# A gated mix of two attentions on one core: roundings moved from ScalarE to GpSimd, copies left out, an eleventh query buffer, and single buffers for the output sums

## The chip, the cores and the metric

The kernel runs on one core of a Trainium2 chip. The metric is the device time of one execution, in microseconds (us). Before the change three runs took 1471.78, 1472.81 and 1473.0 us; their median, 1472.81 us, is the time before. The engines are named as the profile names them: PE (TensorE matmul) and PEld (its weight loads), DVE (VectorE), ACT (ScalarE), POOL (GpSimd) and SP (SyncE, which here only issues DMAs). Each engine works through its own instructions in the order in which they were written.

## The reference, cut to what matters

```python
# x: 1 x 2048 x 512, 32 heads of 16
g = sigmoid((x * gate_w).sum(-1, keepdims=True))
# A: each query sees 8 keys: its own position and 2, 4, ... 14 before it
qkv = x @ A_wqkv;  attn = softmax(q . k[idx] / 4, over 8);  a = (attn . v[idx]) @ A_wo
# B: full softmax attention, 32 query heads, one key head and one value head
q = x @ B_wq; k = x @ B_wk; v = x @ B_wv
p = softmax(q @ k.T / 4);  b = (p @ v) @ B_wo
return g * a + (1 - g) * b
```

## The kernel before

Projections run in the matmul's rounded float type (F32R). A factor is split into a high part, which is its rounding, and a low part, which is the rest; three products (high by high, high by low, low by high) stand for the full one. The PE array is used as two halves of 64 rows, and two matmuls, one on each half, run side by side.

**Front** (up to about 278 us). It loads x and the weights, forms the keys `kst`, and then streams 78 projections ("lumps") of 24 half matmuls each: 14 of queries (two more are done ahead), then 64 of branch A, 16 row blocks for each of four column groups `gg`. A query lump ends in `queries_post`: ACT copies the bank to `qraw` (L221, one buffer) and rounds it into `qhi` (L222, three buffers), POOL forms `qlo` (L229, two buffers), and SP stores both parts to the scratch tensor `qd` (L210). `stack` reads them back into one of the query buffers `qst` (ten of them: NB = 9, and `qstx`). A lump of branch A ends in `a_post`: ACT copies the bank into `stage` (L250, two buffers of two lumps), SP stores it to `ad` (L259); in the first group ACT also copies the value columns to `vst` (L252) and the gate's column to `gate` (L253). The weights of the next group are split by `split_wa`: ACT rounds (`wah`, L81), POOL subtracts (`wal`, L82). After the first group `gates` forms the sigmoid, and 16 small ACT copies turn it into `gate_t` (L272).

**Maxima.** Branch B needs the largest score of each query ahead of its exponentials. Its work is cut into 32 units of 4 heads by 512 queries; each needs 64 half matmuls of 512 columns ("fills", 2048 in all). They are put between other matmuls in three forms: a single (L322 into `ps` or `po`, reduced by DVE, L356); a pair (two into `pm`, one reduction, L344); and, in the front and in the output phases, a difference (L393 into `pd`, ACT L405, DVE L417 with a sum into `ps` or `po`), which settles two fills. When a unit's fills are done, `shift_a` to `shift_d` write its maximum into its query buffer: DVE turns it, ACT makes `mh` (L435), POOL `ml` (L442), and eight DMAs carry it (L453), in the front all on SP.

**Blocks** (the following 1167 us). There are 512 steps, 16 key tiles for each of 32 units. A step has two `exp_pair`s (two matmuls into `pe`, L465, and one ACT exponential of 128x1024, L471), four `weighted` matmuls on the step before (L480), one pair of fills, and where `singles` asks for it one single. POOL does branch A's attention beside it from about 145 us on (`a_load` reads `ad` into `aext`, L531).

**Output phases**, after steps 271, 399 and 447: each makes four row blocks of the output. `turn` transposes branch A's rows into a bank, ACT copies it to `raw` (L651) and rounds it (L652), POOL subtracts (L659); `out_store` copies the finished bank to `two` (L678), POOL adds its halves (L681), SP stores (L682). Four row blocks are left for the end, where ACT and DVE copy the last one half each (L1318, L1319).

**The planner.** The order of all engines is fixed when the program is built. `clk` holds a planned time for PE, ACT and DVE and `pool` one for POOL; each written instruction moves them on by a constant, and `pick`, `side_fill` and `singles` take a fill where the planned clocks allow it. A change of a planned cost so moves fills.

## Time and profile before

| | |
|---|---|
| median of three runs | 1472.81 us |
| the profiled execution | 1471.12 us, span 1469.1 us, TensorE clock 1.000 |
| busy: PE, DVE, ACT, POOL | 99%, 78%, 89%, 65% of the span |
| first exponential of the blocks, end of the last | 278.6 us, 1445.3 us |
| 1024 exponentials of 128x1024 (L471) | 987.8 us in all |

A row of a view of groups reads: line, engine, operation, what is written and read, count, then busy time in us, mean ns of one, idle time of that engine just ahead of them and what ended it. A row of the timeline reads: start in us, length in us, engine, line, operation, written and read, count, and in brackets the idle time ahead of it and its releaser. A row of the waits reads: who waited for whom, us in all, times, longest. PE's ends are modelled, so PE's busy share alone does not say that it was full.

### The profile page before, as it was taken

The numbers are of one execution on the slowest core, as the hardware profiler recorded it, in microseconds if no ns is written. First come the engines' busy times: TensorE is split into PE (matmuls) and PEld (weight loads), VectorE is DVE, ScalarE is ACT, GpSimd is POOL, SyncE is SP. The second block draws the span as 40 slices with busy tenths as digits, with TensorE's granted clock in tenths as the row PEclk, the third lists the DMA queues.
The fourth block names the chain that finished last, engine by engine and source line by source line (L and its number), as shares of the span: only waits on it lengthen the run. The fifth ranks groups of instructions, "written<-read, shape, count | busy, mean of one in ns | idle before, by whom it ended". The sixth has DMA issues, their size and how long they took to land.

```text
span 1469.1 us, 29512 instructions
## 1 busy us (share of the span) xinstructions
PE 1454.6 (99%) x10965; PEld 739.7 (50%) x10965; DVE 1141.9 (78%) x1837; ACT 1303.6 (89%) x1706; POOL 951.1 (65%) x1693
## 2 busy tenths in 40 slices
PE   9999999999999999999999999999999999999998
PEld 6899999733333333333333373333333743383334
DVE  6778888788888888788888877888888778778821
ACT  5888988799999999999999989999999889889994
POOL 5731898888988988889888898898851311150000
PEclk9999999999999999999999999999999999999999
DMA  6653342320211210102202111121100000000000
GB/s 225 170 169 113 101 149 68 117 73 25 71 41 49 78 49 31 68 22 69 78 12 71 42 63 46 45 71 41 42 12 12 27 16 2 1 31 1 1 2 29
DMA packets 43912, 85.67 MB, mean 58 GB/s; under 512 B 9520, under 2 KB 25960, under 8 KB 39672
## 3 DMA queue, kind: packets, MB, share of 16 engines
q1 hardware_dynamic: 36632, 44.79, 9.9%
q0 software_dynamic: 6560, 37.95, 7.7%
q8 instruction: 86, 1.41, 0.4%
q10 hardware_dynamic: 576, 1.05, 0.2%
q14 instruction: 58, 0.48, 0.1%
HBM read 57.97 MB, written 25.25 MB: 57 GB/s over the span
## 4 chain that ended last, share of the span: by engine, by line
PE 94%; ACT 2%; POOL 1%; DVE 1%; DMA 1%; issue 1%; SPq 0%; POOLq 0%; ACTq 0%
PE po L480 34%; PE pe L465 25%; PE pf L1082 10%; PE pm L322 8%; PE ps L322 5%; PE pe L780 5%; PE pd L393 3%; PE po L322 1%; ACT pexp L471 1%; PE pf L193 1%; PE pe L1283 1%; DMA ad<-stage 0%; DVE mx L344 0%; DMA xraw<-xt 0%; PE pm L836 0%
## 5 line engine op out<-in xcount | busy, mean ns | idle before, releaser
L471 ACT ACTIVATE pexp<-pe 128x1024 f32<-128x1024 f32 x1024 | 987.8, 1023 | 67.6 <-PE pe L465 63.3
L344 DVE TENSOR_REDUCE mx<-pm 128x2 f32<-128x1024 f32 x475 | 580.1, 1221 | 174.6 <-PE pm L322 172.3
L480 PE MATMUL po<-pexp,vst 128*32 128x512 f32 x4096 | 545.5, 605 | 0.1
L465 PE MATMUL pe<-qst,kst 64*128 64x512 f32 x1984 | 523.3, 459 | 4.6 <-ACT pexp L471 2.5
L465 PEld LDWEIGHTS pe<-qst,kst 64*128 64x128 f32 x1984 | 208.8, 183 | 451.6 <-ACT pexp L471 427.2
L405 ACT ACTIVATE dd<-pd 128x512 f32<-128x512 f32 x367 | 209.0, 604 | 44.7 <-PE pd L393 30.9
L356 DVE TENSOR_REDUCE mx<-ps 128x1 f32<-128x512 f32 x333 | 226.5, 680 | 4.5 <-PE ps L322 1.8
L322 PE MATMUL ps<-kst,qst 62*128 62x512 f32 x503 | 206.5, 410 | 0.1
L322 PE MATMUL pm<-kst,qst 62*128 62x512 f32 x916 | 185.9, 397 | 0.4
L542 POOL TENSOR_TENSOR pr<-aext 128x256 f32<-128x256 f32 x256 | 182.0, 737 | 4.9 <-DMA aext<-ad 4.6
L602 POOL TENSOR_TENSOR oa<-oa,av 128x256 f32<-128x256 f32 x224 | 164.1, 732 | 15.8
L480 PEld LDWEIGHTS po<-pexp,vst 128*32 128x32 f32 x4096 | 80.6, 108 | 170.3 <-issue 161.8
L417 DVE CUSTOM_DVE_ANT_0 dd<-ps,dd 128x512 f32<-128x512 f32 x185 | 127.7, 690 | 34.2 <-PE ps L322 14.2
L417 DVE CUSTOM_DVE_ANT_0 dd<-po,dd 128x512 f32<-128x512 f32 x182 | 125.6, 690 | 29.8 <-PE po L322 12.9
L599 POOL TENSOR_TENSOR av<-aext,lg 128x256 f32<-128x256 f32 x224 | 139.3, 622 | 12.8
L393 PE MATMUL pd<-kd,qst 62*128 62x512 f32 x367 | 143.5, 401 | 2.5 <-ACT dd L405 2.5
L1082 PE MATMUL pf<-wal,xh 64*128 64x384 f32 (+1 forms) x496 | 127.9, 338 | 0.0
L1082 PE MATMUL pf<-wah,xh 64*128 64x384 f32 (+1 forms) x496 | 124.0, 337 | 0.0
L1082 PE MATMUL pf<-wah,xl 64*128 64x384 f32 (+1 forms) x496 | 122.7, 338 | 0.0
L322 PEld LDWEIGHTS ps<-kst,qst 62*128 62x128 f32 x503 | 92.9, 185 | 43.5 <-DVE mx L356 38.6
L506 POOL TENSOR_TENSOR rl<-rl,gate_t 128x16 f32<-128x16 f32 x31 | 6.9, 222 | 157.9 <-DVE rl L500 157.9
L322 PEld LDWEIGHTS pm<-kst,qst 62*128 62x128 f32 x916 | 88.3, 186 | 3.5 <-DVE mx L344 3.0
(199 smaller groups left out, 1725.4 us busy)
## 6 DMA issues: line engine op xcount, KB each, us to landing
aext<-ad POOLq DMA_DIRECT2D x32, 1056.0 KB, 5.4
ad<-stage SPq DMA_DIRECT2D x32, 384.0 KB
qst<-qd SPq DMA_DIRECT2D x62, 128.0 KB
xraw<-xt SPq DMA_DIRECT2D x16, 256.0 KB
qd<-qhi SPq DMA_DIRECT2D x16, 256.0 KB
qd<-qlo SPq DMA_DIRECT2D x16, 256.0 KB
qst<-qd SPq DMA_DIRECT2D x62, 64.0 KB
qst<-ml SPq DMA_DIRECT2D x220, 2.0 KB
```

The source lines that it names most:

```text
L322: nc.tensor.matmul(dst, qst[place(v)][b:b + 62, pr, t * P:(t + 1) * P], kst[b:b + 62, kc * 512:(kc + 1) * 512], start=True, stop=True)
L344: got = nc.vector.tensor_reduce(m[:, :, pr, t, kc], dst, AX.X, ALU.max)
L356: got = nc.vector.tensor_reduce(m[:, odd, pr, t, kc:kc + 1], dst, AX.X, ALU.max)
L393: nc.tensor.matmul(dst, qst[place(v)][b:b + 62, pr, t * P:(t + 1) * P], kd[0][b:b + 62, kc // 2, :], start=True, stop=True)
L405: got = nc.scalar.activation(held[b][k], dst, AF.Relu)
L417: got = nc.vector.tensor_tensor_reduce(held[b][k], dst, held[b][k], 1.0, -FMAX, ALU.add, ALU.max, m[:, b, pr, t, kc:kc + 1])
L465: nc.tensor.matmul(bank[:, odd, :], kst[b:b + 64, kt * P:(kt + 1) * P], qst[place(u)][b:b + 64, pr, :], start=True, stop=True)
L471: got = nc.scalar.activation(e, bank, AF.Exp, scale=SCALE)
L480: nc.tensor.matmul(po[32 * i:32 * i + 32, :], vst[:, kt, :], pexp[s, i // 2][:, i % 2, :], start=(kt == 0), stop=(kt == NJ - 1))
L542: nc.gpsimd.tensor_mul(pr[:, k], q, e[:, o:o + NH, AC:2 * AC])
L602: nc.gpsimd.tensor_add(ao, ao, av)
L1082: inst = nc.tensor.matmul(home(x)[0][:, :n], l[h], r[h], start=(i == 0 and b == 0), stop=(i == 3 * C - 1 and b == 1))
```

## The change

- `split_wa`: the rounding of the 16 weight pieces moves from ACT to POOL, ahead of POOL's subtraction; the planned cost is 1800 ns, not 1100.
- `queries_post`: ACT only copies the bank to `qraw`; POOL rounds it into `qhi` and then subtracts. The planned cost is 0.62 us on ACT, not 1.1, and 2300 ns on POOL, not 1400.
- `a_post` and `gates`: value and gate columns are copied together into `vst`, the sigmoid reads its column from there, and POOL sets that column back to ones. The 16 copies to `gate_t` become 16 DMAs on SP, and `gate_t` has another layout, which its three readers follow.
- A query buffer `qsty` is allocated at the start of the blocks; `place` and `gone` count with eleven, and the stack of unit 10 moves to step 2.
- `turn`: no copy to `raw`; DVE subtracts, straight out of the bank in PSUM.
- `two` and `os` have one buffer in place of two; the splits of the output weights are written ahead of the next load.
- LEAD is 1.75 for 1.5; the last row block is copied by ACT alone.

```diff
-        split(wah[gg][:, c, :n], wal[gg][:, c, :n], waraw.pop((gg, c))[:, :n], nc.gpsimd)
-        pool = max(pool, clk["pe"] * 1e3) + 1100
+        hi, lo, src = wah[gg][:, c, :n], wal[gg][:, c, :n], waraw.pop((gg, c))[:, :n]
+        nc.gpsimd.tensor_copy(hi, src)
+        nc.gpsimd.tensor_sub(lo, src, hi.bitcast(F32))
+        pool = max(pool, clk["pe"] * 1e3) + 1800
...
-        nc.scalar.activation(hi, bank, AF.Copy)
-        at = after("act", clk["pe"] + T_LAT, 1.1)
-        mark(got, at - 0.45, ups_at)
+        at = after("act", clk["pe"] + T_LAT, 0.62)
+        mark(got, at, ups_at)
...
+            nc.gpsimd.tensor_copy(hi, own)
             nc.gpsimd.tensor_sub(lo, own, hi.bitcast(F32))
-            pool = max(pool, 1e3 * at) + 1400
+            pool = max(pool, 1e3 * at) + 2300
...
-            nc.scalar.activation(vst[:, j, 0:DH], bank[:, GN:GN + DH], AF.Copy)
-            nc.scalar.activation(gate[:, 1, j:j + 1], bank[:, GN + DH:GN + DH + 1], AF.Copy)
-        at = after("act", clk["pe"] + T_LAT, 0.5 if gg else 0.9)
+            nc.scalar.activation(vst[:, j, 0:DH + 1], bank[:, GN:GN + DH + 1], AF.Copy)
+        at = after("act", clk["pe"] + T_LAT, 0.5 if gg else 0.7)
...
-        nc.scalar.activation(gate[:, 0, :], gate[:, 1, :], AF.Exp, scale=-1.0)
+        nc.scalar.activation(gate[:, 0, :], vst[:, :, DH], AF.Exp, scale=-1.0)
+        nc.gpsimd.memset(vst[:, :, DH:DH + 1], 1.0)
...
-        nc.scalar.activation(gate_t[i:i + 32, :, :, b], gate[32 * b:32 * b + 32, 1, :].rearrange("p (q j) -> p q j", j=4), AF.Copy)
-        after("act", 0, 0.24)
+        nc.sync.dma_start(gate_t[i:i + 32, b], gate[32 * b:32 * b + 32, 1, :])
...
-        return v if v <= NB else (v - NB - 1) % (NB - 2)
+        return v if v <= NB + 1 else (v - NB - 2) % (NB - 2)
...
-        return v - NB - 1 if v < 2 * NB - 1 else v - NB + 2
+        return v - NB - 2 if v < 2 * NB else v - NB + 2
...
-        own = pe[0].tile([P, 2, C, 64], F32, name="raw", bufs=1)
-        nc.scalar.activation(own, src, AF.Copy)
         nc.scalar.activation(hv, src, AF.Copy)
-        free[f"e{k}"] = after("act", at, 1.3)
+        ready = after("act", at, 0.65)
...
-            nc.gpsimd.tensor_sub(lv, own, hv.bitcast(F32))
-            pool = max(pool, 1e3 * clk["act"]) + 1300
+            nc.vector.tensor_sub(lv, src, hv.bitcast(F32))
+            free[f"e{k}"] = after("dve", ready + 0.1, 0.74) + 0.1
...
-        two = p2b[0].tile([P, 2, D], F32, name="two", bufs=2)
+        two = p2b[0].tile([P, 2, D], F32, name="two", bufs=1)
...
+    qst.append(pe[0].tile([P, 2, 512], F32R, name="qsty"))
+    clear(NB + 1, nc.gpsimd)
...
-        elif k < 3:
+        else:
             nc.scalar.activation(os, banks[k], AF.Copy)
-        else:
-            nc.scalar.activation(os[:, 0:256], banks[k][:, 0:256], AF.Copy)
-            nc.vector.tensor_copy(os[:, 256:512], banks[k][:, 256:512])
```

The lower planned cost on ACT moves fills. Counted in the order of the PE queue, 576 of the 2048 fills stand ahead of the first exponential before and 606 after; the steps hold 323 singles before and 291 after; the three output phases hold 185 fills before and 184 after, and the rest are pairs. The phases stay at steps 271, 399 and 447. The number of matmuls is the same.

The first place is PE in step 137, the tenth of unit 8. Before (`pe` are the banks of the exponentials, `pm` takes a pair and `ps` a single, `po` sums the weighted values of the step ahead):

```order
L480 MATMUL po_88<-pexp_4273,vst_72 32x512 x2
L480 MATMUL po_88<-pexp_4300,vst_72 32x512 x2
L465 MATMUL pe0_4182<-qst8_84,kst_71 128x512 x2
L322 MATMUL pm_4178<-kst_71,qst4_80 128x512 x2
L322 MATMUL ps_87<-kst_71,qst4_80 128x512
L465 MATMUL pe1_4183<-qst8_84,kst_71 128x512 x2
```

The step holds a pair and a single. After, the same step on PE:

```order
L481 MATMUL po_88<-pexp_4311,vst_72 32x512 x2
L481 MATMUL po_88<-pexp_4351,vst_72 32x512 x2
L466 MATMUL pe0_4228<-qst8_84,kst_71 128x512 x2
L323 MATMUL pm_4224<-kst_71,qst4_80 128x512 x2
L466 MATMUL pe1_4229<-qst8_84,kst_71 128x512 x2
```

The step has lost its single; over all steps 32 singles fewer are left.

The second place is POOL in the front, from the first streamed query lump on. Before (`qst` rows are the clearing of query buffers, `waraw` the load of a weight piece):

```order
L229 TENSOR_TENSOR qlo_375<-qraw_373,qhi_374 128x512
L163 MEMSET qst4_80 32x1024 x2
L229 TENSOR_TENSOR qlo_429<-qraw_427,qhi_428 128x512
L163 MEMSET qst5_81 32x1024 x2
L131 DMA waraw_492<-wa 128x402
L229 TENSOR_TENSOR qlo_489<-qraw_487,qhi_488 128x512
```

After, on the same queue:

```order
L230 CAST qhi_374<-qraw_373 128x512
L231 TENSOR_TENSOR qlo_375<-qraw_373,qhi_374 128x512
L165 MEMSET qst4_80 32x1024 x2
L230 CAST qhi_427<-qraw_426 128x512
L231 TENSOR_TENSOR qlo_428<-qraw_426,qhi_427 128x512
L165 MEMSET qst5_81 32x1024 x2
L131 DMA waraw_486<-wa 128x402
L230 CAST qhi_483<-qraw_482 128x512
L231 TENSOR_TENSOR qlo_484<-qraw_482,qhi_483 128x512
```

A CAST stands ahead of each subtraction; the clearings stay where they were.

The third place is SP at the shift of unit 5, in branch A's third column group. Before (`ml` rows carry a unit's maximum, `stage` rows store projections):

```order
L259 DMA ad_69<-stage_2833 128x4x192
L453 DMA qst5_81<-ml_2934 2x8x32 x4
L259 DMA ad_69<-stage_2935 128x4x192
L453 DMA qst5_81<-ml_2934 2x8x32 x4
L259 DMA ad_69<-stage_3045 128x4x192
```

After, where POOL issues the next `aext` load directly behind its `ml`:

```order
L260 DMA ad_69<-stage_2772 128x4x192
L454 DMA qst5_81<-ml_2799 2x8x32 x8
L260 DMA ad_69<-stage_2878 128x4x192
L260 DMA ad_69<-stage_2984 128x4x192
L260 DMA ad_69<-stage_3081 128x4x192
```

All eight DMAs of the shift now stand ahead of the next store. The 16 DMAs to `gate_t` stand on SP among the shifts of units 3 and 4 and the stores around them.

More of the change, by code (lines that the diff above doesn't have):

```diff
@@ L41 @@
 NH = NJ // 2
-LEAD, M2S, M1S, MARGIN = 1.5, 0.5, 0.3, 0.12
+LEAD, M2S, M1S, MARGIN = 1.75, 0.5, 0.3, 0.12
 T_R, T_LAT, T_EXP, T_RED2, T_RED1, T_W, T_TTR = 0.235, 0.20, 0.92, 1.14, 0.61, 1.21, 0.74
@@ L63, in gated_mix_kernel @@
     gate = cp.tile([P, 2, NJ], F32, name="gate")
-    gate_t = cp.tile([P, NQB, 4, 4], F32, name="gate_t")
+    gate_t = cp.tile([P, 4, NJ], F32, name="gate_t")
     mk = cp.tile([P, 8], F32, name="mk")
@@ L505, in finish_b @@
             charge(950)
-        eng.tensor_mul(rl, rl, gate_t[:, qb].rearrange("p j b -> p (j b)"))
+        rv = rl.rearrange("p (j b) -> p j b", b=4)
+        eng.tensor_mul(rv, rv, gate_t[:, :, 4 * qb:4 * qb + 4].rearrange("p b j -> p j b"))
         eng.tensor_mul(obp["t"][:, :, hg % 2, :], tt[:, :, 0:DH], rl.unsqueeze(2).to_broadcast([P, 4 * 4, DH]))
@@ L622, in wo_load @@
     def wo_load(k, c):
-        wot[k, c] = p2b[0].tile([P, 512], F32, name="os", tag="two", bufs=2)
+        wot[k, c] = p2b[0].tile([P, 512], F32, name="os", tag="two", bufs=1)
         nc.sync.dma_start(wot[k, c], (wo_a, wo_b)[k][c * P:(c + 1) * P, :])
@@ L947, in gated_mix_kernel @@
     for i in range(2 * C + 1):
[L948 to L949 removed]
+        wos.append([(wo_split, kcs[i - 1])] if i else [])
+        wos[-1] += [(wo_load, kcs[i])] if i < 2 * C else []
     def work():
@@ L1229, in gated_mix_kernel @@
         u, kt = divmod(s, NJ)
-        if len(stacked) < NU and s >= 16 * (gone(len(stacked)) + 1):
+        if len(stacked) < NU and s >= max(2, 16 * (gone(len(stacked)) + 1)):
             stack(len(stacked))
```

11 lines of the change are left out of this document (5 added, 6 removed).

## The prediction, made before the changed kernel was run

> **What bounds the kernel now.** I read the page first.
>
> ```profile
> PE 1454.6 (99%) x10965; PEld 739.7 (50%) x10965; DVE 1141.9 (78%) x1837; ACT 1303.6 (89%) x1706; POOL 951.1 (65%) x1693
> ...
> PE 94%; ACT 2%; POOL 1%; DVE 1%; DMA 1%; issue 1%; SPq 0%; POOLq 0%; ACTq 0%
> ```
>
> PE is busy throughout and holds 94% of the chain. But its ends are modelled, so the next view is the busy time by stage: a stretch with POOL's early work, one of branch A's projections, and one of the blocks.
>
> ```profile
> 24.00:60.00 36.00, 35.74 (x267) 30.36 (x267) 28.81 (x69) 27.64 (x53) 32.19 (x30) 1.00 0.55 154
> ...
> 100.00:146.00 46.00, 46.00 (x477) 45.76 (x476) 37.56 (x114) 38.55 (x102) 7.33 (x13) 1.00 0.34 106
> 500.00:600.00 100.00, 100.00 (x705) 35.91 (x708) 81.90 (x100) 94.37 (x104) 87.80 (x174) 1.00 0.13 43
> ```
>
> In the front (second row) weights load for 45.76 of 46 us while ACT and DVE have idle time: PE is the limit. In the blocks PE and ACT (94.37) are both near full, so I look at single steps there. These rows are the starts of five steps on PE, and the waits name what ACT lacks:
>
> ```profile
> 501.02 0.50 PE L465 MATMUL pe<-qst,kst 64*128 64x512 f32 x2
> ...
> 503.20 0.50 PE L465 MATMUL pe<-qst,kst 64*128 64x512 f32 x2
> ...
> 505.35 0.50 PE L465 MATMUL pe<-qst,kst 64*128 64x512 f32 x2
> ...
> 507.24 0.50 PE L465 MATMUL pe<-qst,kst 64*128 64x512 f32 x2
> ...
> 509.37 0.50 PE L465 MATMUL pe<-qst,kst 64*128 64x512 f32 x2
> ```
>
> ```profile
> ACT pexp L471 <- PE pe L465: 63.3, 279, 1.7
> ```
>
> The steps take 2.18, 2.15, 1.89 and 2.13 us. The third alone holds no single fill; there ACT runs its two exponentials without a gap. A single makes the step wait for PE. So fills cost differently by place, and the change moves them.
>
> **The change, part by part.**
>
> *Singles out of the blocks.* 323 become 291, 32 fewer. The waits price one: 63.3/279 = 0.227 us of idle ACT. 32 x 0.227 = 7.3 us less. The four steps give 2.153 - 1.89 = 0.26, or 8.3, as the far end. The near end comes from ACT's small work, which the idle time in steps with a single can hide:
>
> ```profile
> L435 ACT ACTIVATE mh<-mt,mk 128x32 fp32r<-128x32 f32 x32 | 10.4, 325 | 0.1
> ...
> L572 ACT ACTIVATE lg<-lg 128x128 f32<-128x128 f32 x32 | 10.0, 311 | 0.0
> ```
>
> If 32 of 512 steps no longer hide it, 20.4 x 32/512 = 1.3 us show, so 6.0. I take 7.3, the price over 279 cases.
>
> *More fills in the front.* 576 become 606, 30 more, between matmuls that already fill PE. The groups of 100 to 146 us:
>
> ```profile
> L1082 PE MATMUL pf<-wah,xl 64*128 64x402 f32 x86 | 22.8, 342 | 0.0
> ...
> L393 PE MATMUL pd<-kd,qst 62*128 62x512 f32 x54 | 21.3, 394 | 0.0
> L1082 PE MATMUL pf<-wah,xh 64*128 64x384 f32 x38 | 10.9, 335 | 0.0
> ...
> L322 PE MATMUL po<-kst,qst 62*128 62x512 f32 x27 | 10.7, 396 | 0.0
> ...
> L1082 PE MATMUL pf<-wah,xl 64*128 64x384 f32 x36 | 9.5, 335 | 0.0
> ```
>
> There are three groups of 86 with 402 columns, 54 + 27 + 27 fills with 512 (the two 27 read alike), and 111 matmuls with 384 (groups of 38, 37 and 36), 201,636 columns in 46 us. A fill takes 512/201,636 of that, 0.117 us, as two halves run at once. 30 x 0.117 = +3.5 us. The ends are +2 (some fall into gaps) and +7 (each keeps the other half idle).
>
> *ACT relieved in the front.* The groups that go or shrink:
>
> ```profile
> L222 ACT ACTIVATE qhi<-pf 128x512 fp32r<-128x512 f32 x14 | 8.4, 598 | 0.0
> ...
> L81 ACT ACTIVATE wah<-waraw 128x384 fp32r<-128x384 f32 (+1 forms) x16 | 8.6, 537 | 0.1
> ...
> L272 ACT ACTIVATE gate_t<-gate 32x16 f32<-32x16 f32 x16 | 3.6, 228 | 0.4
> ```
>
> That is 20.6 us off an engine that is not the limit: worth nothing beyond the fills it lets in, priced above.
>
> *Rounding on POOL.* 14 query roundings and 16 weight roundings are added to a queue that was busy for 32.19 of 36 us between 24 and 60 us. ACT may write `qraw` again only when POOL has subtracted, so POOL's pace now counts. Its rows, with the cast's duration from the end of the kernel, a weight subtraction, and two ACT copies:
>
> ```profile
> 37.71 1.29 POOL L229 TENSOR_TENSOR qlo<-qraw,qhi 128x512 fp32r<-128x512 f32 x1
> 39.05 1.93 POOL L163 MEMSET qst<- 32x1024 f32 x2
> ...
> 44.30 0.62 POOL L131 DMA_DIRECT2D waraw<-wa  x1
> ```
>
> ```profile
> L803 POOL CAST qst<-ob x3: 609/611/613, 1222.0 to 1387.9; 128x512 fp32r<-128x512 f32 x3
> ```
>
> ```profile
> L82 POOL TENSOR_TENSOR wal<-waraw,wah 128x384 fp32r<-128x384 f32 (+1 forms) x16 | 15.2, 949 | 34.6 <-ACT wah L81 34.6
> ```
>
> ```profile
> 39.03 0.60 ACT L221 ACTIVATE qraw<-pf 128x512 f32<-128x512 f32 x1
> ...
> 59.59 0.59 ACT L221 ACTIVATE qraw<-pf 128x512 f32<-128x512 f32 x1
> ```
>
> POOL's first pair now ends at 37.7 + 0.61 + 1.29 = 39.6, so the second copy, due at 39.03, waits 0.6. Up to the sixth pair POOL has six pairs (11.4), five clearings (9.7), two loads (1.2) and one weight pair (0.95 and 402/512 of a cast, 1.4): it ends at 61.4, where the seventh copy was due at 59.59. Later the clearings are over and POOL catches up. I take +1.5 us, between 0 (PE has four banks to run ahead in) and +2.2. The second group's weight roundings have room (POOL was busy for 7.33 of 46 us); the later ones, with a planned cost above their own, defer branch A's work instead of being late.
>
> The Trainium skill (SBUF — State Buffer, on the port that VectorE and GpSimd share) says that a VectorE instruction in a two-port mode, or with two SBUF inputs, shuts a GpSimd instruction out until it ends. By that a cast could take longer than 0.61; the three casts here, within 4 ns of each other in a stretch where DVE is busy, don't show it.
>
> *The stores behind the shifts.* The front's one long stall:
>
> ```profile
> 205.34 0.25 POOL L442 TENSOR_TENSOR ml<-mt,mh 128x32 fp32r<-128x32 f32 x1
> ...
> 207.92 0.57 POOL L531 DMA_DIRECT2D aext<-ad  x1
> ```
>
> ```profile
> 205.62 2.61 SPq L453 DMA_DIRECT2D qst<-ml  x4
> 208.34 0.36 SPq L259 DMA_DIRECT2D ad<-stage  x1
> ```
>
> ```profile
> 215.56 0.49 ACT L250 ACTIVATE stage<-pf 128x384 f32<-128x384 f32 x1 [2.94 <-DMA ad<-stage]
> ```
>
> SP's four DMAs waited for a late `ml`; the store behind them was issued 0.4 us after a load into `aext` and landed 7.2 us later, and ACT stood for 2.94 us. In the new order the store stands behind eight DMAs, planned later in the row pair, and POOL's branch A work is deferred, so `ml` should be less late. I take the stall as gone, less 0.6 for the gate DMAs on SP (one such ahead of a store, 2.61/4): -2.3, with ends -2.9 and +2.9 (one more of its kind).
>
> *Phases and end.* `two` has one buffer:
>
> ```profile
> 859.67 1.03 ACT L678 ACTIVATE two<-pe 128x1024 f32<-128x1024 f32 x1 [0.19 <-PE pd L393]
> ...
> 867.85 1.03 ACT L678 ACTIVATE two<-pe 128x1024 f32<-128x1024 f32 x1
> ```
>
> ```profile
> 862.93 0.37 SPq L682 DMA_DIRECT2D out<-two  x1
> ```
>
> The store has 4.9 us to land before the next copy. I count nothing; if it took the 7.2 us seen above, the copy would be 2.3 us late. The Trainium skill (Trainium Kernel Development and Optimization, Best Practices) asks for double buffers to overlap DMA with compute and so speaks against this part. In `turn` ACT and POOL lose an instruction each and DVE gets four subtractions a phase:
>
> ```profile
> L818 DVE TENSOR_TENSOR qst<-pm,qst x4: 691/692/693, 1400.7 to 1406.7; 128x512 fp32r<-128x512 f32 x4
> ...
> 1464.70 0.38 ACT L1318 ACTIVATE osl<-ps 128x256 f32<-128x256 f32 x1 [4.60 <-PE ps L1310]
> ...
> 1465.12 0.42 DVE L1319 COPY osl<-ps 128x256 f32<-128x256 f32 x1 [6.27 <-ACT osl L1318]
> ```
>
> 4 x 0.69 = 2.8 us a phase lie beside PE's work, with fills as many as before (185, now 184): 0, ends -1 and +2.8. The two halves of the last copy ran one behind the other, 0.84 us; one copy of 512 columns takes 0.60 (L221 above): -0.2. The eleventh buffer, the order of the weight splits and LEAD move no phase: 0.
>
> *Sum*: -7.3 + 3.5 + 1.5 - 2.3 - 0.2 = -4.8. The profiled execution took 1471.12, below all three timed runs, so 1466.3 in its terms; on their median of 1472.81 it is **1468.0 us**. I call 0.2%, 2.9 us, the least that a measurement tells from no change; faster then means under 1469.9, slower over 1475.7.
>
> **The rivals.**
>
> *The gain is eaten.* The stage stall recurs once (no -2.3) and POOL's queue costs its upper end: -7.3 + 3.5 + 2.2 - 0.2 = -1.8, 1471.0. For it: the pattern of late `ml`, SP, and store is all still there. Against: POOL's deferred work.
>
> *Slower by stores behind shifts.* If late shifts and gate DMAs push the store in front of the second, third and fourth group into `aext` loads, each costs 2.94. Without the -2.3 the sum is -2.5 with one such stall, as before; two make +0.4, three +3.4, which is 1476.2. It decides from three on. For it: six shifts fall into this stretch. Against: the trace has one.
>
> *Casts held up.* If each cast waits for one DVE instruction of 0.69, the seventh copy is 6 x 0.69 = 4.1 us later: -4.8 + 4.1 = -0.7, 1472.1. The Trainium skill's page SBUF — State Buffer would make this case.
>
> *One sum buffer waits.* If every store lands only after 7.2 us, the three copies of each phase that have a predecessor wait 2.3 us: 9 x 2.3 = 20.7, 1488.7. Such a landing was seen only beside a large load, and two of the phases come after those. The Trainium skill's Best Practices (Trainium Kernel Development and Optimization) would make this case.
>
> **How the numbers follow.** Forecast 0.60; gain eaten 0.24; casts held up 0.05; three stalls 0.08; sum buffer 0.03. Faster is the forecast, 0.60; same is the two middle ones, 0.29; slower 0.11. The range for 8 in 10 leaves out the last two and a little below: its upper end, 1473.5, holds the eaten gain and the held casts with some spread; its lower end, 1463.5, is the forecast with singles at 8.3, the front's fills at +2, and the queue at 0 (4 us less) and a little spread.
>
> **What would show it.** Exponentials should start about 3 us later or less than before; ACT's wait for PE ahead of exponentials should have some 250 cases, not 279; the query copies should wait for `qlo`, below 2 us each; the wait for the stage store should be gone; the copies into `two` should wait for no DMA. I am wrong if the first exponential comes more than 6 us later, if the steps without a single take longer than 1.9 us, or if the copy into `two` waits for a DMA.

## The result, and the profile after

The changed kernel took 1466.63 us (median of six runs, 1465.39 to 1469.46) beside 1472.89 us before (six runs, 1470.65 to 1473.33): a ratio of 0.9962, with a 95% interval of 0.9952 to 0.9972. A second set of five runs gave 1467.31 us and 0.9968 (0.9955 to 0.9980). So it is faster by 0.3 to 0.4% (0.2 to 0.5% by the intervals); 1468.0 us was forecast. Two executions, one of experiment 9 (1553.73 us at a clock of 0.85) and one of the kernel before (2234.95 us at 0.56), were slow and are left out of every ratio.

The first profiled run took 1469.46 us, the longest of its six, with a granted clock of 0.997. The second took 1466.83 us at 0.999, and it is the one read here unless said otherwise. Its page:

```profile
PE 1452.1 (99%) x10965; PEld 741.2 (51%) x10965; DVE 1140.7 (78%) x1844; ACT 1294.1 (88%) x1647; POOL 956.5 (65%) x1714
...
PE 92%; POOL 2%; ACT 1%; issue 1%; DVE 1%; DMA 1%; SPq 0%; POOLq 0%; ACTq 0%
```

ACT's busy time fell by 9.5 us, POOL's rose by 5.4, and PE holds 92% of the chain, where it held 94%. Three spans add up to the difference of the two profiled executions, 4.1 us. The first exponential starts here, before the change and then after it:

```profile
278.56 1.03 ACT L471 ACTIVATE pexp<-pe 128x1024 f32<-128x1024 f32 x1 [0.72 <-PE pe L465]
```

```profile
280.88 1.03 ACT L472 ACTIVATE pexp<-pe 128x1024 f32<-128x1024 f32 x1 [1.06 <-PE pe L466]
```

| us | before | after | difference |
|---|---|---|---|
| start to first exponential | 278.6 | 280.9 | +2.3 |
| first exponential to the end of the last | 1166.7 | 1160.75 | -6.0 |
| end of the last exponential to the end | 23.8 | 23.4 | -0.4 |

(The first profile had +2.6, -3.7 and -0.4.) The front became longer, and the blocks won more. What ACT waits for, in a view of the waits after:

```profile
ACT pexp L472 <- PE pe L466: 55.5, 248, 1.4
...
ACT qraw L223 <- POOL qlo L231: 4.4, 4, 2.5
...
ACT stage L252 <- DMA ad<-stage: 4.2, 4, 2.1
```

In the first row, 279 cases and 63.3 us have become 248 and 55.5: 31 fewer, at 0.224 us each. The second row is POOL's queue, which hardly held ACT before (0.4 us, once). The third is the stall that the prediction had as gone: there are four of them now (one, of 1.5 us, in the first profile).

**A ledger of the front.** The prediction had a pace for PE there, 46 us for 201,636 columns. What a stretch takes beyond its columns at that pace is its shortfall. All 78 lumps are the same in every kernel; only the fills differ. The stretches run from the first query copy to the first stage copy (query lumps), from there to the 17th stage copy (first group), and to the 57th (later groups). Each cell has fills / length / shortfall, worked out from the records of PE and ACT in one trace of each kernel.

| | query lumps | first group | later groups | shortfall |
|---|---|---|---|---|
| before | 125 / 55.9 / 1.9 | 111 / 48.2 / 0.2 | 304 / 125.3 / 5.5 | 7.6 |
| changed | 140 / 58.3 / 2.6 | 124 / 51.1 / 1.6 | 306 / 122.1 / 2.2 | 6.4 |
| old planned costs | 125 / 58.5 / 4.5 | 111 / 48.2 / 0.2 | 304 / 124.6 / 4.9 | 9.6 |
| queries rounded on ACT | 125 / 54.9 / 1.1 | 126 / 50.3 / 0.2 | 305 / 121.1 / 1.4 | 2.7 |
| the same, order of the changed | 140 / 59.4 / 3.8 | 124 / 51.5 / 1.9 | 306 / 122.1 / 2.2 | 7.9 |
| before, queries rounded on POOL | 140 / 59.3 / 3.7 | 111 / 49.8 / 1.7 | 305 / 123.6 / 3.9 | 9.3 |
| weights rounded on ACT | 140 / 59.3 / 3.7 | 124 / 51.3 / 1.8 | 306 / 123.2 / 3.1 | 8.6 |

Busy time by stretch shows the same. Before the change, 34 to 74, 74 to 145 and 145 to 245 us (columns: PE, PEld, DVE, ACT, POOL, clock, DMA share, GB/s):

```profile
34.00:74.00 40.00, 39.77 (x332) 35.56 (x331) 30.95 (x88) 34.48 (x68) 30.21 (x33) 1.00 0.58 160
74.00:145.00 71.00, 71.00 (x714) 69.47 (x714) 57.29 (x174) 60.43 (x151) 17.24 (x24) 1.00 0.45 138
145.00:245.00 100.00, 97.70 (x1006) 94.88 (x1004) 84.63 (x254) 87.83 (x184) 87.10 (x173) 1.00 0.37 114
```

After it:

```profile
34.00:74.00 40.00, 38.95 (x323) 32.61 (x322) 32.91 (x94) 31.47 (x59) 36.58 (x44) 1.00 0.57 157
74.00:145.00 71.00, 69.90 (x690) 67.79 (x688) 61.01 (x182) 58.69 (x129) 22.18 (x34) 1.00 0.41 119
145.00:245.00 100.00, 100.00 (x1041) 98.19 (x1043) 87.88 (x264) 86.03 (x165) 88.22 (x166) 1.00 0.40 125
```

PE lost 0.8 us in the first stretch and 1.1 in the second, and won 2.3 in the third; the weight loads (PEld) went from 94.88 to 98.19 of 100 us there.

### The profile page after: what moved, and what is told of

Read it like the earlier page. It is cut to its first block, busy times and chain, and to the rows that moved or that the text cites. A ratio compares the mean times of both kernels' runs of the same rounds, so it can differ in the third digit from the quotient of the medians.

```text
span 1467.7 us, 29483 instructions
## 1 busy us (share of the span) xinstructions
PE 1453.2 (99%) x10965; PEld 741.7 (51%) x10965; DVE 1140.8 (78%) x1844; ACT 1293.9 (88%) x1647; POOL 954.3 (65%) x1714
## 4 chain that ended last, share of the span: by engine, by line
PE 92%; POOL 3%; issue 2%; ACT 1%; DVE 1%; DMA 1%; SPq 0%; POOLq 0%; ACTq 0%
PE po L481 33%; PE pe L466 24%; PE pf L1083 10%; PE pm L323 8%; PE ps L323 5%; PE pe L781 4%; PE pd L394 3%; PE po L323 2%; ACT pexp L472 1%; POOL xl L82 1%; PE pe L1286 1%; DVE mx L345 0%; DMA xraw<-xt 0%; POOL tr L550 0%; DMA ad<-stage 0%
## 5 line engine op out<-in xcount | busy, mean ns | idle before, releaser
L466 PE MATMUL pe<-qst,kst 64*128 64x512 f32 x1920 | 497.5, 461 | 5.3 <-ACT pexp L472 3.1
L466 PEld LDWEIGHTS pe<-qst,kst 64*128 64x128 f32 x1920 | 197.4, 184 | 446.6 <-ACT pexp L472 415.3
L406 ACT ACTIVATE dd<-pd 128x512 f32<-128x512 f32 x382 | 222.5, 601 | 52.9 <-PE pd L394 27.8
L357 DVE TENSOR_REDUCE mx<-ps 128x1 f32<-128x512 f32 x302 | 205.5, 680 | 3.6 <-PE ps L323 3.1
L323 PE MATMUL ps<-kst,qst 62*128 62x512 f32 x467 | 191.0, 409 | 0.3 <-DVE mx L418 0.2
L418 DVE CUSTOM_DVE_ANT_0 dd<-ps,dd 128x512 f32<-128x512 f32 x193 | 133.1, 690 | 28.3 <-ACT dd L406 7.8
L1083 PE MATMUL pf<-wal,xh 64*128 64x384 f32 (+1 forms) x496 | 148.0, 338 | 0.0
L418 DVE CUSTOM_DVE_ANT_0 dd<-po,dd 128x512 f32<-128x512 f32 x189 | 130.4, 690 | 19.7 <-PE po L323 9.4
L1083 PE MATMUL pf<-wah,xh 64*128 64x384 f32 (+1 forms) x496 | 145.5, 338 | 0.0
L1083 PE MATMUL pf<-wah,xl 64*128 64x384 f32 (+1 forms) x496 | 141.8, 337 | 0.0
L323 PEld LDWEIGHTS ps<-kst,qst 62*128 62x128 f32 x467 | 86.7, 186 | 32.0 <-DVE mx L357 26.1
L1083 PEld LDWEIGHTS pf<-wal,xh 64*128 64x128 f32 x496 | 90.8, 186 | 0.2
```

The source lines that it names most:

```text
L323: nc.tensor.matmul(dst, qst[place(v)][b:b + 62, pr, t * P:(t + 1) * P], kst[b:b + 62, kc * 512:(kc + 1) * 512], start=True, stop=True)
L357: got = nc.vector.tensor_reduce(m[:, odd, pr, t, kc:kc + 1], dst, AX.X, ALU.max)
L406: got = nc.scalar.activation(held[b][k], dst, AF.Relu)
L418: got = nc.vector.tensor_tensor_reduce(held[b][k], dst, held[b][k], 1.0, -FMAX, ALU.add, ALU.max, m[:, b, pr, t, kc:kc + 1])
L466: nc.tensor.matmul(bank[:, odd, :], kst[b:b + 64, kt * P:(kt + 1) * P], qst[place(u)][b:b + 64, pr, :], start=True, stop=True)
L1083: inst = nc.tensor.matmul(home(x)[0][:, :n], l[h], r[h], start=(i == 0 and b == 0), stop=(i == 3 * C - 1 and b == 1))
```

## The experiments

Edits are against the changed kernel unless said otherwise. (The expectations count 190 fills in the output phases of the changed kernel, where the count above has 184: they take in one pair beside each phase.)

**1. The changed kernel once more.** 

> The changed kernel itself, profiled once more. The first profile of it had a TensorE clock of 0.997 and was the longest of its runs (1469.46 us against a median of 1466.63); in it the stretch from the first to the last exponential was only 3.7 us shorter than before (1163.0 against 1166.7), where the prediction had 7.3 for the singles taken out. Theory 1 (each single taken out of the blocks is worth 0.227 us of ACT waiting for PE): at a clock of 1.000 that stretch is 7 us shorter than before, 1159.5, and the first exponential stays at 281.2. Rival (ACT's small work eats half of it): the stretch stays at 1162 to 1163 and the missing 3 us come from the front, whose first exponential is then at 278 to 279.

Measured: 1467.31 us, the blocks 1160.75, the first exponential at 280.88. That is Theory 1's front, and blocks between the two, nearer to Theory 1. Five other kernels with 291 singles bound it: their blocks took 1159.4, 1159.8, 1160.2, 1160.6 and 1161.8 us (experiments 6, 7, 12, 9 and 8, the last with a clock of 0.997), 4.9 to 7.4 less than before.

**2. Old planned costs, new operations.**

```diff
-        at = after("act", clk["pe"] + T_LAT, 0.62)
-        mark(got, at, ups_at)
+        at = after("act", clk["pe"] + T_LAT, 1.1)
+        mark(got, at - 0.45, ups_at)
...
-            pool = max(pool, 1e3 * at) + 2300
+            pool = max(pool, 1e3 * at) + 1400
```

(1800 and 0.7 in `split_wa` and `a_post` went back to 1100 and 0.9 as well.) 

> The changed kernel with the planner's old costs (1.1 us on ACT and 1400 ns on POOL for a query lump, 0.9 us for a lump of the first branch A group, 1100 ns for a weight piece). All operations stay those of the changed kernel, so ACT, POOL and the stores are relieved or loaded as in it; only fills move: 578 in the front for 606, 307 singles in the blocks for 291, 964 fills in pairs for 961, 199 in the output phases for 190. Theory 1 (fills moved): -28 x 0.117 = -3.3 us in the front, +16 x 0.227 = +3.6 in the blocks, +9 x 0.117 = +1.1 in the phases, so +1.4 us, 1468.0; the first exponential is 3.3 us earlier than in the changed kernel, at 278. ACT's waits for PE ahead of exponentials have some 268 cases, not 254. Rival (the relief of ACT itself is worth something and the front's fills are free): the front stays as long as in the changed kernel, 281, and the time is 1466.6 + 3.6 + 1.1 = 1471.3.

Measured: 1472.02 us, ratio 1.0001 (0.9992 to 1.0010): the whole gain is gone although every operation is the changed one. The first exponential is at 281.69, where Theory 1 had 278. The time is the rival's, but not its reason: the ledger shows 30 fills fewer, worth 3.5 us, and 3.2 us more shortfall (9.6 for 6.4), so the front gains nothing, and the blocks take 1165.1 us, 4.4 more. In the query lumps POOL rounds, and a plan that takes it for faster than it is runs into it: a query copy waits 2.90 us for POOL, up to 58.43 us, and PE pauses for 2.0 us of the 10 between 50 and 60. What holds PE back in the later groups (4.9 short for 2.2) was not followed. The stretches:

```profile
34.00:74.00 40.00, 38.00 (x306) 34.20 (x304) 28.75 (x82) 27.28 (x51) 36.05 (x44) 0.96 0.58 156
74.00:145.00 71.00, 71.00 (x710) 70.22 (x709) 57.40 (x172) 56.00 (x126) 23.96 (x36) 1.00 0.44 125
145.00:245.00 100.00, 97.50 (x1014) 95.08 (x1012) 85.38 (x257) 82.58 (x161) 89.58 (x178) 1.00 0.39 121
```

The first row has a clock of 0.96; it was 0.83 between 60 and 70 us, which may account for up to 0.17 x 10 = 1.7 us of that stretch's shortfall.

**3. Without the eleventh buffer.**

```diff
-        return v if v <= NB + 1 else (v - NB - 2) % (NB - 2)
+        return v if v <= NB else (v - NB - 1) % (NB - 2)
...
-        return v - NB - 2 if v < 2 * NB else v - NB + 2
+        return v - NB - 1 if v < 2 * NB - 1 else v - NB + 2
...
-    qst.append(pe[0].tile([P, 2, 512], F32R, name="qsty"))
-    clear(NB + 1, nc.gpsimd)
...
-        if len(stacked) < NU and s >= max(2, 16 * (gone(len(stacked)) + 1)):
+        if len(stacked) < NU and s >= 16 * (gone(len(stacked)) + 1):
```

> The changed kernel without the eleventh query buffer (placement and stacking times as before the change). The front keeps its 606 fills; the blocks have 301 singles for 291, 944 fills in pairs for 961, 197 in the phases for 190. The prediction counted the buffer as nothing by itself. Theory 1 (fills moved): +10 x 0.227 + 7 x 0.117 = +3.1 us, 1469.7, with the first exponential at the same time and some 263 waits of ACT for PE. Rival (only the front's fills matter): no change, 1466.6.

Measured: 1471.40 us, 0.9992 (0.9983 to 1.0001). The front is the same (281.07; shortfall 6.4), the blocks take 1165.15. So 10 singles more and 17 fills fewer in pairs go with 4.1 us, more than the 3.1 forecast, and without this buffer next to nothing of the gain remains.

**4. LEAD at 1.5.**

```diff
-LEAD, M2S, M1S, MARGIN = 1.75, 0.5, 0.3, 0.12
+LEAD, M2S, M1S, MARGIN = 1.5, 0.5, 0.3, 0.12
```

> The changed kernel with LEAD at 1.5 as before the change. The prediction said that LEAD moves no phase; in fact with 606 fills in the front the third output phase then comes after step 463 and not 447, and the blocks have 277 singles for 291, 963 fills in pairs for 961, 197 in the phases for 190. Theory 1 (fills moved): -14 x 0.227 + 7 x 0.117 = -2.4 us, 1464.2, unless the later phase comes too late for the end. Rival (a phase 16 steps later hands its wait to the end or loses its fills): 1467 to 1470.

Measured: 1471.67 us, 1.0000 (0.9991 to 1.0008). Theory 1 missed by 7.5 us. From the first exponential up to the end of the second phase the two traces agree within 0.3 us; then the third phase comes 16 steps later, and the fills that it would have taken are due before it:

```profile
1301.41 1.22 PE L466 MATMUL pe<-qst,kst 64*128 64x512 f32 x4 [1.77 <-DVE mx L345]
1302.25 1.94 ACT L472 ACTIVATE pexp<-pe 128x1024 f32<-128x1024 f32 x2 [5.17 <-PE pe L466]
```

Ahead of this step, 456, the planner's `pause` writes fills into the exponentials' own banks; the step takes 7.11 us, and ACT waits 5.17. So the kernel before has its third phase at step 447 with a LEAD of 1.5, but with the new fills it takes 1.75 to keep it there, and that is worth some 4 us.

**5. Query roundings back on ACT.**

```diff
-        at = after("act", clk["pe"] + T_LAT, 0.62)
-        mark(got, at, ups_at)
+        nc.scalar.activation(hi, bank, AF.Copy)
+        at = after("act", clk["pe"] + T_LAT, 1.1)
+        mark(got, at - 0.45, ups_at)
...
-            nc.gpsimd.tensor_copy(hi, own)
             nc.gpsimd.tensor_sub(lo, own, hi.bitcast(F32))
-            pool = max(pool, 1e3 * at) + 2300
+            pool = max(pool, 1e3 * at) + 1400
```

> The changed kernel with the query roundings back on ACT, at their old planned costs (1.1 us on ACT, 1400 ns on POOL); everything else stays. The order then has 592 fills in the front for 606, 301 singles in the blocks for 291, 964 fills in pairs for 961. The changed kernel took 1466.6 and 1467.3 us. Theory 1 (fills moved, and PE held up by POOL in the query lumps): -14 x 0.117 = -1.6 in the front, -1.1 for PE time that the longer POOL queue cost between 34 and 74 us, +10 x 0.25 = +2.5 in the blocks: -0.2, so 1466.8, with the first exponential near 278.2 and no wait of a query copy for POOL above 0.5 us. Rival (it is the rounding's leaving ACT that brought the gain): 1470 to 1472.

Measured: 1464.58 us (five runs, 1464.30 to 1466.14), 0.9950 (0.9938 to 0.9962): the lowest of all versions. Four of its five runs lie below all eleven of the changed kernel, though the intervals of the two ratios overlap. The first exponential is at 275.48, 5.4 us before the changed kernel's; the blocks take 1163.64, 2.9 more, for ten singles more. Its stretches:

```profile
34.00:74.00 40.00, 39.98 (x337) 36.69 (x336) 31.32 (x91) 34.22 (x68) 32.11 (x36) 1.00 0.62 168
74.00:145.00 71.00, 71.00 (x713) 69.37 (x711) 60.49 (x184) 59.98 (x136) 18.93 (x30) 1.00 0.43 132
145.00:245.00 100.00, 100.00 (x1050) 99.36 (x1048) 88.00 (x265) 85.32 (x167) 91.15 (x181) 1.00 0.38 115
```

PE hardly pauses. Fourteen fills fewer explain 1.6 us of the front and the shortfall (2.7 for 6.4) the rest. In the first group PE streams 9,234 columns more than before (15 fills, and a few matmuls of a lump at the edge of the stretch) in 2.12 us more (50.3 for 48.2), both 0.2 short: 2.12 x 512/9,234 = 0.118 us for a fill, beside the forecast 0.117.

**6. Clearings further apart.**

```diff
-        tasks.append((37.0 + 3.5 * (k - 4), clear, (k, nc.gpsimd)))
+        tasks.append((37.0 + 5.5 * (k - 4), clear, (k, nc.gpsimd)))
```

> The changed kernel with the five clearings of query buffers on POOL planned 5.5 us apart, not 3.5; no fill moves (606, 291, 961, 190 as in the changed kernel). The copies of queries wait 4.4 us for POOL in all there, and PE fell 2.6 us behind its pace between 34 and 74 us, against 1.5 before the change. Theory 1 (POOL's queue costs 1.1 us because the clearings stand in it): the waits fall below 2 us, the first exponential comes 1 us earlier, at 280, and the time is 1 us less, 1465.9. Rival (PE's four banks hide the queue, the lost time has another reason): no change in the waits' effect, 1466.9.

Measured: 1465.86 us. The number is Theory 1's, the trace is the rival's: the first exponential is at 281.11, the query lumps fall 2.7 us short (2.6 in the changed kernel), and the waits stay:

```profile
ACT qraw L223 <- POOL qlo L231: 4.2, 4, 2.5
```

Its time lies within the changed kernel's own runs. So a wider distance of the clearings changes nothing that these runs can tell; the longest wait, 2.49 us, is over before the first clearing starts. What a queue without them would cost was not run.

**7. ACT's relief undone: weight roundings and gate copies back on ACT.**

```diff
-        hi, lo, src = wah[gg][:, c, :n], wal[gg][:, c, :n], waraw.pop((gg, c))[:, :n]
-        nc.gpsimd.tensor_copy(hi, src)
-        nc.gpsimd.tensor_sub(lo, src, hi.bitcast(F32))
-        pool = max(pool, clk["pe"] * 1e3) + 1800
+        split(wah[gg][:, c, :n], wal[gg][:, c, :n], waraw.pop((gg, c))[:, :n], nc.gpsimd)
+        pool = max(pool, clk["pe"] * 1e3) + 1100
...
-        nc.sync.dma_start(gate_t[i:i + 32, b], gate[32 * b:32 * b + 32, 1, :])
+        nc.scalar.activation(gate_t[i:i + 32, b], gate[32 * b:32 * b + 32, 1, :], AF.Copy)
+        after("act", 0, 0.24)
```

> The changed kernel with the 16 weight roundings back on ACT (537 ns each) and the 16 copies of the gate back on ACT (228 ns each) in place of DMAs: 12.2 us more work on ACT in the front, 16 DMAs fewer on SP. The order has 607 fills in the front for 606, 291 singles, 954 fills in pairs for 961, 196 in the output phases for 190. Theory 1 (ACT's relief is worth nothing where PE is the limit): 0 + 6 x 0.117 = +0.7, 1467.7, less up to 1.2 if the gate DMAs are what holds the stage store up at 107 us. Rival (ACT's relief in the front is worth something): up to 12 us more in the front, 1470 or above.

Measured: 1470.10 us, 0.9985 (0.9976 to 0.9994), the first exponential at 285.12. The rival holds: ACT's relief is worth something, 2.8 us beside the second set of the changed kernel.

**8. Stage stores issued by ACT.**

```diff
-            tasks.append((at + 0.3, lambda: nc.sync.dma_start(dst[:, :, (j - 1) * AN:(j + 1) * AN], st.rearrange("p g j n -> p g (j n)")), (), "store"))
+            tasks.append((at + 0.3, lambda: nc.scalar.dma_start(dst[:, :, (j - 1) * AN:(j + 1) * AN], st.rearrange("p g j n -> p g (j n)")), (), "store"))
```

> The changed kernel with the stores of the stage tiles issued by ACT, not by SP, so that none stands behind the DMAs of a shift. No fill moves. In the second profile of the changed kernel ACT waits for such a store at 106.5 us (1.57 us; PE pauses 1.2) and at 284 us, after the first exponential (2.07 us). Theory 1 (the stall was not removed by the change but moved, by SP's order): both waits go, -1.2 in the front and -1.5 to -2 at the start of the blocks, 1464 us. Rival (the store lands late for its own sake, as beside the loads that POOL issues): the waits stay, 1467; and if ACT's issues (0.35 us each, 32 of them) hold up its copies, 1468 to 1470.

Measured: 1477.18 us, 1.0031 (1.0019 to 1.0043): both theories missed. ACT no longer waits for `ad<-stage`, but it stands elsewhere:

```profile
ACT dd L406 <- DMA qst<-ml: 6.2, 2, 3.8
```

```profile
180.08 0.37 ACTq L260 DMA_DIRECT2D ad<-stage  x1
180.55 1.09 ACT L406 ACTIVATE dd<-pd 128x512 f32<-128x512 f32 x2 [3.78 <-DMA qst<-ml]
```

A shift's transfers, which the store stood behind on SP, now hold ACT at the store's issue, with its fills behind it, and the front is 9.4 us longer. The trace shows what the issue waits for: a semaphore, the counter by which a transfer's landing is told. It is the one that this store will use, and the transfer that used it last was a shift's DMA, issued by SP at 178.34 us. ACT stood still in this way ahead of five stores, for 1.0 to 3.3 us each; the last user of the semaphore was a shift's DMA four times and a read-back of queries once, issued by SP 1.7 to 5.3 us earlier.

**9. Query roundings on ACT, in the changed kernel's order.** As 5, but with ACT's planned cost left alone:

```diff
+        nc.scalar.activation(hi, bank, AF.Copy)
         at = after("act", clk["pe"] + T_LAT, 0.62)
...
-            nc.gpsimd.tensor_copy(hi, own)
             nc.gpsimd.tensor_sub(lo, own, hi.bitcast(F32))
-            pool = max(pool, 1e3 * at) + 2300
+            pool = max(pool, 1e3 * at) + 1400
```

> The changed kernel with the query roundings on ACT, but with ACT's planned cost left at 0.62 us, so that the order of the fills is that of the changed kernel (606 in the front, 291 singles, 961 in pairs, 190 in the phases); ACT really needs 1.2 us there. Beside the run with the old planned cost (1464.6 us, 592 fills and 301 singles) it prices fills alone, beside the changed kernel (1466.6 and 1467.3) the place of the rounding alone. Theory 1 (fills cost 0.117 us in the front, singles 0.27 in the blocks, and POOL's queue of the changed kernel costs PE 1.7 us between 34 and 74 us, with the late stores of the stage after it): +1.6 - 2.7 = -1.1 against 1464.6, so 1463.5, with the first exponential near 277. Rival (ACT falls behind its plan in the query lumps and PE waits for it, as it did for POOL): 1466 to 1468, the first exponential at 279 to 281.

Measured: 1468.1 us, 0.9974 (0.9963 to 0.9985), the first exponential at 282.32: the rival. With 140 fills in the query lumps ACT falls behind too (3.8 us short, POOL 2.6); with 125 it keeps up (1.1). So the order that the low planned cost brings, not the engine alone, makes that stretch late. The fourth case, POOL with the order of experiment 5, was not run; the nearest is experiment 2 (POOL, 125 fills, 4.5 short, up to 1.7 of it by the clock).

**10. The kernel before, with query roundings on POOL alone.** Against the kernel before:

```diff
-        nc.scalar.activation(hi, bank, AF.Copy)
-        at = after("act", clk["pe"] + T_LAT, 1.1)
-        mark(got, at - 0.45, ups_at)
+        at = after("act", clk["pe"] + T_LAT, 0.62)
+        mark(got, at, ups_at)
...
+            nc.gpsimd.tensor_copy(hi, own)
             nc.gpsimd.tensor_sub(lo, own, hi.bitcast(F32))
-            pool = max(pool, 1e3 * at) + 1400
+            pool = max(pool, 1e3 * at) + 2300
```

> The kernel before with one part of the change alone: the query roundings on POOL, with the new planned costs (0.62 us on ACT, 2300 ns on POOL). The order then has 594 fills in the front for 576, 301 singles in the blocks for 323, 957 fills in pairs for 958, 196 in the phases for 191. Theory 1 (fills moved, POOL's queue costs PE time): +18 x 0.117 = +2.1 in the front, +1.1 to +3.3 for POOL's queue, -22 x 0.25 = -5.5 in the blocks, +0.6 in the phases: -1.7 to +0.5 against 1472.2, so 1471.5. Rival (the moved rounding is what brought the gain of the whole change): 1467 to 1468.

Measured: 1471.05 us, 0.9993 (0.9984 to 1.0002), as Theory 1 had it. The first exponential is at 282.72 and the blocks take 1163.54: 4.2 us lost in the front, 3.2 won.

**11. The old `turn`.**

```diff
...
+        own = pe[0].tile([P, 2, C, 64], F32, name="raw", bufs=1)
+        nc.scalar.activation(own, src, AF.Copy)
         nc.scalar.activation(hv, src, AF.Copy)
-        ready = after("act", at, 0.65)
+        free[f"e{k}"] = after("act", at, 1.3)
...
-            nc.vector.tensor_sub(lv, src, hv.bitcast(F32))
-            free[f"e{k}"] = after("dve", ready + 0.1, 0.74) + 0.1
+            nc.gpsimd.tensor_sub(lv, own, hv.bitcast(F32))
+            pool = max(pool, 1e3 * clk["act"]) + 1300
...
```

> The changed kernel with the old transposition step: ACT copies the bank to a raw tile and rounds it, POOL subtracts. The order has 606 fills in the front as in the changed kernel, 294 singles for 291, 964 fills in pairs for 961, 184 in the phases for 190. The prediction counted this part as nothing, with ends -1 and +2.8. Theory 1: +3 x 0.25 - 6 x 0.117 = 0, 1467, and phases of the same length (36.8, 37.1, 36.2 us for the two steps that hold them). Rival (DVE's four subtractions a phase lie on the path, or ACT's copies did): a difference of 1 us or more a phase, 3 us in all.

Measured: 1467.91 us, as Theory 1. The two steps that hold a phase take 36.5, 36.0 and 36.9 us (36.8, 37.1 and 36.2 in the changed kernel; 37.3, 36.2 and 36.6 before).

**12. Weight roundings alone back on ACT.** The first half of 7's edit:

```diff
-        nc.gpsimd.tensor_copy(hi, src)
-        nc.gpsimd.tensor_sub(lo, src, hi.bitcast(F32))
-        pool = max(pool, clk["pe"] * 1e3) + 1800
+        split(wah[gg][:, c, :n], wal[gg][:, c, :n], waraw.pop((gg, c))[:, :n], nc.gpsimd)
+        pool = max(pool, clk["pe"] * 1e3) + 1100
```

> The changed kernel with the 16 weight roundings alone back on ACT (537 ns each, 8.6 us); the gate DMAs stay. Fills: 606, 291, 955 in pairs for 961, 196 in the phases for 190. With both these roundings and the gate copies back the time was 1470.1 us, and PE fell 3.3 us further behind its pace between 74 and 245 us, where the prediction had counted nothing for ACT's relief. If the weights bring that about (they run through the groups up to 245 us): 1469 to 1470, with the loss of PE's pace in the same places. If the gate copies do (they run from 145 us on, for some 50 us): 1467 to 1467.7.

Measured: 1469.57 us, 0.9988 (0.9979 to 0.9997), the first exponential at 283.80. The weights hold most of what 7 lost (2.3 of 2.8 us beside the second set). Their planned cost on POOL went back with them, and the two were not separated. The stretches:

```profile
34.00:74.00 40.00, 39.30 (x325) 32.71 (x323) 33.05 (x93) 31.33 (x60) 34.79 (x40) 1.00 0.57 155
74.00:145.00 71.00, 69.42 (x680) 65.93 (x678) 60.04 (x177) 59.78 (x132) 20.42 (x29) 1.00 0.41 118
145.00:245.00 100.00, 99.77 (x1028) 96.64 (x1027) 87.21 (x265) 87.36 (x173) 86.32 (x171) 1.00 0.40 126
```

The weight loads lose 1.9 us in the second stretch and 1.6 in the third. Which instruction is late behind each rounding was not followed.

## Why the prediction was right, and where its steps were wrong

The mechanism holds: fills were moved from places where they cost 0.22 us to places where they cost 0.12. The forecast difference was -4.8; the second profile gave -4.3 (the first -1.7) and the medians -6.3 and -5.1. But two terms of the front were wrong, the stores and ACT's relief, and they nearly cancelled. That the front came out at +2.3 beside a forecast of 3.5 + 1.5 - 2.3 = +2.7 is in part luck.

| term | forecast | measured |
|---|---|---|
| singles out of the blocks | -7.3 (-6.0 to -8.3) | -6.0; -4.9 to -7.4 in five other kernels; -3.7 in the first profile (clock 0.997) |
| 30 more fills in the front | +3.5 | +3.5 by the ledger's pace, which the first group of experiment 5 bears out |
| rounding on POOL | +1.5 | +0.7 (query lumps 1.9 to 2.6 short), net of ACT's relief there; +1.8 in experiment 10 |
| stage stores behind shifts, gate DMAs | -2.3 | +1.4 in the first group; part of -3.3 in the later ones |
| ACT relieved | 0 | the rest of that -3.3, and some in the query lumps (3.7 short in experiment 12) |
| phases, sum buffers | 0 | 110.1 us for the three, 110.1 before |
| last copy | -0.2 | -0.4 at the end |

In the front the measured column adds up to 3.5 + 0.7 + 1.4 - 3.3 = +2.3. By the lengths themselves the three stretches grew by 2.1 us; the time ahead of them is 0.3 shorter and the time from them to the first exponential 0.5 longer, which makes the +2.3 of the first exponential. How the later groups' -3.3 divides between the stall that went and ACT's relief was not separated.

**Singles.** The price was right: 0.227 us a case before, 0.224 after, and 0.217 to 0.236 in the other traces (0.243 in experiment 4, with its one wait of 5.17 us). The cases are not one to one with singles (31 fewer here; 17 fewer in experiment 10, for 22 singles). The steps show it directly: with a single they have a median of 2.14 us, without one 1.90 us, before the change and after it alike (323 and 291 steps with a single). So the steps without a single did not become longer, which would have been a sign of being wrong. The means are 0.21 us apart, and 32 x 0.21 = 6.7 us lies between the forecast 7.3 and the measured 6.0.

**"The stores behind the shifts": wrong.** The stall at 215 us went and another came, in the first group. In the first profile it reads:

```profile
107.09 0.49 ACT L252 ACTIVATE stage<-pf 128x384 f32<-128x384 f32 x1 [1.50 <-DMA ad<-stage]
```

SP's issues ahead of it, in the second profile:

```profile
95.05 1.40 SPq L454 DMA_DIRECT2D qst<-ml  x2
96.56 0.60 SPq L291 DMA_DIRECT2D qstx<-qd  x1
97.21 0.56 SPq L292 DMA_DIRECT2D qstx<-qd  x1
97.83 0.58 SPq L291 DMA_DIRECT2D qstx<-qd  x1
98.45 0.57 SPq L292 DMA_DIRECT2D qstx<-qd  x1
99.06 3.99 SPq L454 DMA_DIRECT2D qst<-ml  x6
103.16 6.93 SPq L260 DMA_DIRECT2D ad<-stage  x3
```

Twelve DMAs of 0.6 to 0.7 us each are issued ahead of the first store. And SP, done with the last query store at 92.9, first waits 2.1 us for `ml`, which stands on POOL behind a clearing:

```profile
92.43 1.94 POOL L165 MEMSET qstx<- 32x1024 f32 x2
...
94.77 0.26 POOL L443 TENSOR_TENSOR ml<-mt,mh 128x32 fp32r<-128x32 f32 x1
```

The lump that completes the store's tile was copied by 95.9 us; the store is issued 7.3 us later. In experiment 5 the first store stands behind two of the shift's DMAs, and nothing waits:

```profile
92.21 1.41 SPq L454 DMA_DIRECT2D qst<-ml  x2
93.72 0.40 SPq L260 DMA_DIRECT2D ad<-stage  x1
94.17 3.90 SPq L454 DMA_DIRECT2D qst<-ml  x6
```

So the pattern that I had named in the rivals, late `ml`, SP and store, is what happened, at a place that I had not looked at: there the new order has the store behind all eight of the shift's DMAs, where the kernel before had it behind three. The gate DMAs, which I had charged 0.6 us, come later. The last of the four waits, 2.07 us long, lies behind the first exponential; the next exponential comes 3.9 us after the first, as before the change, so that one is covered.

**"ACT relieved in the front: 0": wrong.** I read it off the stretch from 100 to 146 us, where weights loaded for 45.76 of 46 us. That holds for the first group alone: in the later groups they loaded for 94.88 of 100 us and in the query lumps for 35.56 of 40 (36.69 in experiment 5), and there ACT's work was in the way. Experiments 7 and 12 put 2 to 3 us on it.

**Rounding on POOL.** One sign failed here, that no query copy waits for 2 us; and the longest wait comes at the second copy, not at the seventh. The first profile:

```profile
39.64 0.60 ACT L223 ACTIVATE qraw<-pf 128x512 f32<-128x512 f32 x1 [2.48 <-POOL qlo L231]
...
48.29 0.60 ACT L223 ACTIVATE qraw<-pf 128x512 f32<-128x512 f32 x1 [0.74 <-POOL qlo L231]
...
56.88 0.60 ACT L223 ACTIVATE qraw<-pf 128x512 f32<-128x512 f32 x1 [0.18 <-POOL qlo L231]
62.52 0.60 ACT L223 ACTIVATE qraw<-pf 128x512 f32<-128x512 f32 x1 [0.99 <-POOL qlo L231]
```

The second copy waited 2.48 us, not 0.6: in the new order it was due earlier than its 39.03 of before. No clearing stands ahead of it; POOL first has four subtractions for x:

```profile
32.54 5.14 POOL L82 TENSOR_TENSOR xl<-xraw,xh 128x512 fp32r<-128x512 f32 x4
37.61 0.62 POOL L230 CAST qhi<-qraw 128x512 fp32r<-128x512 f32 x1
38.32 1.29 POOL L231 TENSOR_TENSOR qlo<-qraw,qhi 128x512 fp32r<-128x512 f32 x1
```

The seventh waited 0.99, not 1.8. The ledger's +0.7 is no measure of the term, as ACT's relief is in it: with the weights still on ACT (experiment 10) the query lumps fall 1.8 us further short than before, near the forecast 1.5. The order counts as much as the engine: on ACT these lumps were 1.1 us short with 125 fills and 3.8 with 140, on POOL 4.5 (up to 1.7 by the clock) and 2.6. The chance of casts held up by DVE can be struck off (a row of the groups, first profile):

```profile
L230 POOL CAST qhi<-qraw 128x512 fp32r<-128x512 f32 x14 | 8.5, 610 | 6.6 <-ACT qraw L223 6.3
```

The mean is 610 ns, as in the three casts of before. The Trainium skill (SBUF — State Buffer, Who interferes with whom) would have let these casts stand behind VectorE instructions with two inputs in SBUF. Beside them VectorE's two-input work (L418) has one input in PSUM (`po` or `ps`), so that case does not arise, and the casts show no hold.

**One sum buffer.** In the first phase of the first profile the copies stand 7.3 to 8.2 us apart, and none waits for a DMA:

```profile
859.44 1.03 ACT L679 ACTIVATE two<-pe 128x1024 f32<-128x1024 f32 x1
867.61 1.02 ACT L679 ACTIVATE two<-pe 128x1024 f32<-128x1024 f32 x1
...
882.45 1.02 ACT L679 ACTIVATE two<-pe 128x1024 f32<-128x1024 f32 x1 [1.78 <-PE pe L781]
```

Only experiment 11 has such a wait, 0.4 us, once. In the second profile the stores had 4.5 to 5.8 us from their issue to the next copy. Its view of the waits leaves 4.2 us ahead of four copies without a cause; each ends within 0.2 us of the last matmul into the bank that is copied, so PE is the likely one. So the double buffer that the Trainium skill asks for (Trainium Kernel Development and Optimization, Best Practices) was not needed at this distance between uses. Two sum buffers beside the eleventh query buffer were not run.

**"The eleventh buffer and LEAD: 0": wrong as a price.** The buffer moves no phase; its effect is in the count of singles (301 without it, 291 with it), and the prediction didn't name it as a cause of that count. LEAD does move a phase once the new fills are there (experiment 4). Without either one the kernel is back at 1471.4 to 1471.7 us. The gain is that of parts together; old costs, one buffer fewer or the old LEAD each cost nearly all of it.

## What to carry to other kernels

Where a planner sets the order, a planned cost is an edit of its own: experiment 2 lost the whole gain by numbers alone, and experiment 9 shows a cost set too low for the engine that does the work. Whether relief of an engine is worth something is read stretch by stretch, since one full stretch of PE says nothing of the next; a ledger of columns at PE's own pace shows what PE's busy time does not (39.77 of 40 us before the change, in query lumps that fell 1.9 us short). Undo each part of a change that gains: here the rounding of the queries, with its planned cost, was the part to leave out.

## What the runs showed of the hardware

DMAs issued one behind the other on SP took 0.56 to 0.70 us each: twelve of them made 8 us, enough to hold up a store behind them. Stores issued on ACT in place of SP cost more than the stall that they were to remove (+9.4 us in the front); ACT stood still until an earlier transfer, which shared the store's semaphore, had landed (up to 3.3 us). A cast of 128x512 on POOL kept to 610 ns and a subtraction to 1.30 us with POOL and DVE both busy. A half matmul of 512 columns added to a full stretch took 0.118 us.
